# Transposing V by 32-bit words in the backward part of a fused decode block

## The chip, the cores and the metric

The kernel runs on one core of a Trainium2 chip (trn2). The metric is the device time of one execution in microseconds. Engines are named as in the profile: PE is TensorE (PEld its weight loads), DVE is VectorE, ACT is ScalarE, POOL is GpSimd, SP is SyncE, which here issues nearly all DMAs.

## What is computed

A decode step of one transformer block, forward and backward: layer norm, attention over a cache, output projection, layer norm, gated MLP. There are 4 batch rows and 32 attention heads, so 128 pairs of row and head, called heads here and numbered s. Each has a K and a V cache of 4096 x 128 in bf16, 1 MB each. The outputs are the block's output and the gradients of x, of both caches and of the weights. What matters here, for one head:

```
forward:   p  = softmax(q K^T * scale)          # 1 x 4096
           o  = p V
backward:  dP = dO V^T                          # 1 x 4096
           dS = p * (dP - dO.o) * scale
           dK = dS^T q      (4096 x 128, written out)
           dV = p^T dO      (4096 x 128, written out)
```

K is read once, V twice (once forward, once backward), and dK and dV are written once.

## The kernel before

SBUF holds one large tile, the arena, of 23 slots of 4160 bf16 elements for each of 128 partitions. A slot holds a head of K, of V, or of a gradient: 4096 tokens as 128 partitions of 32 tokens, with 128 features each. Slots are taken from a list of free ones when a load or a gradient is set up and given back when it is used or stored. All loads and stores of caches go through SP's queue in the order in which the program writes them.

**Forward, to 660 us.** A loop over 64 groups of 2 heads loads K and V, computes scores and softmax, and builds the sums that the backward needs. It is not touched.

**Middle, 660 to 700 us.** Projection, MLP and their backward for the 4 rows. It ends with dO for the first 8 attention heads (dOT_bf, features on partitions, one column for each head; `dO_columns`, L768, and `dO_rows`, L778) and the first transposes of V (`V_T`, L793).

**Backward, from 700 us.** The first SP = 32 heads are taken one by one (`front`, L1212), the other 96 in NT = 48 pairs (`front_pair`, L1292). In a pair, two heads of one batch row lie in two neighbouring slots, 64 partitions for each head, 64 tokens on a partition, and are loaded with one DMA of 2 MB. For a head or a pair:

1. V is loaded again (`load_V2` L829, `load_pair` L1276).
2. V is transposed on PE in 128 x 128 blocks, one token number of all partitions at a time. Eight blocks fill one PSUM tile, pt_tps, of 128 x 1024 bf16, one bank; one ACT copy takes it back to the same place in SBUF (L800 and L801, L1298 and L1299). psT has two such tiles. A head takes 4 banks, a pair 8.
3. dP comes from matmuls with 32 output rows and 512 columns, four side by side in the array (`tile_position`); the stationary operand is zero but for the column or columns with dO (`zd` for heads, `zt` for pairs), so that each head adds its rows to a shared PSUM tile, dP_ps (L1228, L1313). `dO_window` (L1191) and `dO_pair` (L1287) write dO into zd and zt on POOL, two heads or pairs ahead. After the matmuls the slot of V is given back.
4. After four heads, or two pairs, `rows_out` (L1200, ACT) and `rows_T` (L1205, four f32 transposes on PE) bring dP_ps back to tokens on partitions, in the midst of the next front. `group_dS` (L1239) and `group_dS_pair` (L1319) form dS on DVE.
5. dV and dK are outer products on DVE (L806 for heads, L1379 for pairs) into free slots, and each is stored. Their factors are P or dS, doubled, and dO or q copied to all partitions. The doubled P is made on POOL (`P_pairs` L1195, `P2_pair` L1372), the copies on PE and ACT (`replicate` L1172, `replicate_pair` L1356).

The order is written out by hand in the loops from L1436 on: fronts run 5 heads (L) or 3 pairs (LP) ahead of dK, and dV runs some heads ahead of dK (`more_V`, `lead_V`). Between them `side` (L1428) places the rest: dO of the other heads, dq, the weight gradients (`grad_unit`, L981). SP meets loads and stores in this order and waits at each for its slot or its data.

The two matmul loops for dP take the transposed V like this (L1228 and L1313):

```
lhsT=zq_window(zd[hl], 2 * hl + u), rhs=VT[:, j0:j0 + 4, :]
lhsT=zt[t % B][:, 32 - m:64 - m],   rhs=v[:, j0:j0 + 4, :]
```

Of the kernel before, what the change touches and what calls it, by code (L numbers as in the profile page):

```python
# [9 lines left out]
FP32 = mybir.dt.float32  # L10
BF16 = mybir.dt.bfloat16
# [10 lines left out]
SP = 32  # L22
# [5 lines left out]
def kernel(  # L28
# [22 lines left out]
    nc = tc.nc  # L51
    P = nc.NUM_PARTITIONS

    B = A_x.shape[0]
# [3 lines left out]
    Dh = A_k_cache.shape[3]  # L58
    F = B_w1.shape[1]
    NH = B * H  # L60
# [4 lines left out]
    SJ = Sk // P  # L65
    FC = F // P
    GW = 8
# [13 lines left out]
    while f0 < F:  # L81
        w = min(512, F - f0)
# [125 lines left out]
    for i in range(2):  # L208
        t = fcon.tile([P, 64], BF16, name=f"onesw{i}")
# [132 lines left out]
    def zq_window(z, m):  # L342
        a = 66 * (m % 2) + 32 + (m % 2) - m
        return z[:, a:a + 32]
# [305 lines left out]
    for gi in range(NGI):  # L650
        nxt = gi < NGI - 1
        a, na, nb = gi * G, gi * G + 2, gi * G + 3
# [137 lines left out]
    V2s, VTs = {}, {}  # L790


    def V_T(s, ps, part=range(SJ // GW)):  # L793
        if s not in VTs:
            VTs[s] = V2s.pop(s)
        v = VTs[s].heads()
        for g in part:
            pt = ps.tile([P, GW, P], BF16, tag="tps", name="pt_tps")
            for i in range(GW):
                nc.tensor.transpose(pt[:, i, :], v[:, g * GW + i, :], ident_b[:])  # L800
            nc.scalar.copy(out=v[:, g * GW:(g + 1) * GW, :], in_=pt[:])  # L801

    P2s, first_gv = {}, []

# [160 lines left out]
    with ExitStack() as c2:  # L965
# [218 lines left out]

        rows = {}
        dS2s = {}
        zd = [bw3.tile([P, 132], BF16, name=f"zd{i}", tag=f"zd{i}", bufs=1) for i in range(B)]
        for i in range(B):
            nc.gpsimd.memset(zd[i][:], 0.0)

        def dO_window(s):  # L1191
            if s < SP:
                nc.gpsimd.tensor_copy(out=zd[s % B][:, 32:132:67], in_=dOT_bf[:, s:s + 1].to_broadcast([P, 2]))

        def P_pairs(s):  # L1195
            if s < SP and s not in P2s:
# [15 lines left out]
        def front(s):  # L1212
            hl = s % B
            if s not in VTs:
                for g in range(SJ // GW):
                    V_T(s, psT, range(g, g + 1))
                    if hl == 0 and g == 0:
                        rows_out()
                    if hl == 0 and g == 2:
                        rows_T()  # L1220
            VT = VTs[s].heads()
            if hl == 0:
                rows["acc"] = psD.tile([P, 512], FP32, tag="dP", name="dP_ps")
            dO_window(s + 2)
            for u in range(2):
                for c in range(4):
                    j0 = 8 * c + 4 * u
                    nc.tensor.matmul(rows["acc"][32 * c:32 * (c + 1), :], lhsT=zq_window(zd[hl], 2 * hl + u),  # L1228
                                     rhs=VT[:, j0:j0 + 4, :], start=(hl == 0 and u == 0),
                                     stop=(hl == B - 1 and u == 1), tile_position=(0, 32 * c))  # L1230
            if hl == B - 1:
                rows["ps"] = rows.pop("acc")
            sl = VTs.pop(s)
            if nv["next"] < SP and len(V2s) + len(VTs) + len(vring) < NV2:
                vring.append(sl.i)
            else:
                gave(sl.i, stored=False)

        def group_dS(g):  # L1239
            i0 = g * B  # L1240
            T = rows.pop("T").rearrange("p jj (c m) -> p c m jj", c=4)
            t = rows.pop("t")[:, 0:B * SJ].rearrange("p (b j) -> p b j", b=B)
            t5 = t.rearrange("p b (c u jj) -> p b c u jj", c=4, u=2)
            for hl in range(B):
                nc.vector.tensor_scalar(out=t5[:, hl], in0=T[:, :, 2 * hl:2 * hl + 2, :], scalar1=c_rep[:, i0 + hl:i0 + hl + 1],
                                        scalar2=scale, op0=ALU.subtract, op1=ALU.mult)
# [40 lines left out]
        def dO_pair(t):  # L1287
            if t < NT:
                s, s2 = two(t)
                nc.gpsimd.tensor_copy(out=zt[t % B][:, 32:34], in_=dOT_bf[:, s:s2 + 1:B])  # L1290

        def front_pair(t, mid):  # L1292
            pl = t % 2
            v = pV[t].t[:, 0:2 * SJ * Dh].rearrange("p (j d) -> p j d", d=Dh)
            for g in range(2 * SJ // GW):
                pt = psT.tile([P, GW, P], BF16, tag="tps", name="pt_tps")
                for i in range(GW):
                    nc.tensor.transpose(pt[:, i, :], v[:, g * GW + i, :], ident_b[:])  # L1298
                nc.scalar.copy(out=v[:, g * GW:(g + 1) * GW, :], in_=pt[:])  # L1299
                if pl == 0 and g == 0:  # L1300
                    rows_out()
                if pl == 0 and g == 2:
                    rows_T()
                if g == 3:
                    mid()
            if pl == 0:
                rows["acc"] = psD.tile([P, 512], FP32, tag="dP", name="dP_ps")
            dO_pair(t + 2)
            for u in range(4):
                m = 8 * pl + 2 * u  # L1310
                for c in range(4):
                    j0 = 16 * c + 4 * u
                    nc.tensor.matmul(rows["acc"][32 * c:32 * (c + 1), :], lhsT=zt[t % B][:, 32 - m:64 - m], rhs=v[:, j0:j0 + 4, :],  # L1313
                                     start=(pl == 0 and u == 0), stop=(pl == 1 and u == 3), tile_position=(0, 32 * c))
            if pl == 1:
                rows["ps"] = rows.pop("acc")
            pV.pop(t).give()

        def group_dS_pair(g):  # L1319
            T = rows.pop("T").rearrange("p jj (c z l u a) -> p z l a c u jj", c=4, z=2, l=2, u=4, a=2)  # L1320
            t = rows.pop("t")[:, 0:4 * SJ].rearrange("p (l j) -> p l j", l=2)
            t5 = t.rearrange("p l (c u jj) -> p l c u jj", c=4, u=4)
            for l in range(2):
                for a, s in enumerate(two(2 * g + l)):
                    r_ = slice(64 * a, 64 * (a + 1))
                    nc.vector.tensor_scalar(out=t5[r_, l], in0=T[r_, 0, l, a], scalar1=c_rep[r_, s:s + 1],  # L1326
                                            scalar2=scale, op0=ALU.subtract, op1=ALU.mult)
            pdS[g] = bw3.tile([P, 2, 2 * SJ, 2], BF16, tag="dS2", name="dS2", bufs=1)
            nc.vector.tensor_tensor(out=pdS[g][:], in0=t[:, :, :, None].to_broadcast([P, 2, 2 * SJ, 2]),
                                    in1=P_two(2 * g)[:, :, :, None].to_broadcast([P, 2, 2 * SJ, 2]), op=ALU.mult)  # L1330

        Pp, zt, P2b = {}, [], []

        def P_two(t, n=2):
# [2 lines left out]
        def P_rows(q):  # L1337
            if q >= NT // B or q in Pp:
                return
            if not Pp:  # L1340
                Pp["s"] = Slot("Pp")
                x = Pp["s"].t[:, NT * 2 * SJ:]
                zt.extend(x[:, 66 * i:66 * (i + 1)] for i in range(B))
                nc.gpsimd.memset(x[:, 0:66 * B], 0.0)
                P2b.extend(x[:, n:n + 4 * SJ].rearrange("p (j t) -> p j t", t=2) for n in (66 * B, 66 * B + 4 * SJ))
# [82 lines left out]
        def side(s):  # L1428
# [4 lines left out]
            elif s >= O0:  # L1433
                step("q")

        for s in range(2):  # L1436
            dO_window(s)
        for s in range(3, 6):
# [11 lines left out]
        for s in range(SP):  # L1450
# [73 lines left out]
```

## Time and profile before

| | |
|---|---|
| median of 3 runs | 1697.81 us (1697.64 to 1698.8) |
| span of the profiled execution, first to last instruction | 1696.2 us |
| PE busy, matmuls / weight loads | 1233.4 us (73%) / 943.4 us, 16,228 of each |
| DVE, ACT, POOL busy | 1234.4 us (73%), 959.5 us (57%), 336.9 us (20%) |
| moved by DMA | 707.45 MB, 417 GB/s in the mean |
| transposes of V, pairs (L1298) | 3,072 of 128 x 128, 308.1 us, mean 272 ns |
| their copies (L1299) | 384 of 128 x 1024, 369.8 us, mean 1023 ns |
| transposes of V, heads (L800), copies (L801) | 1,024, mean 229 ns; 128, mean 1025 ns |
| dP matmuls, pairs (L1313), heads (L1228) | 768, mean 484 ns; 256, mean 403 ns |
| f32 transposes in rows_T (L1210) | 128, mean 370 ns; their weight loads 196 ns |
| POOL copies of dO (L1290, L1193) | 48, mean 995 ns; 32, mean 872 ns |

The profile is one execution recorded by the hardware. The span is all of it that has rows; 1.6 us lie between it and the median of the runs. Its page gives busy times by engine, 40 slices of the span, the DMA queues, the chain that ended last, and groups of instructions by source line. A row of a group reads: line, engine, operation, what it writes and reads, shape, count, then busy time and mean of one, then the idle time of the engine before them and who ended it. Slice digits are tenths. The trace behind it also has each DMA packet with queue, start, duration and size, and the landings: every transfer on SP's queue is split over 16 DMA engines, and each reports the end of its share.

### The profile page before, as it was taken

The numbers are of one execution on the slowest core, as the hardware profiler recorded it, in microseconds if no ns is written. First come the engines' busy times: TensorE is split into PE (matmuls) and PEld (weight loads), VectorE is DVE, ScalarE is ACT, GpSimd is POOL, SyncE is SP. The second block draws the span as 40 slices with busy tenths as digits, with TensorE's granted clock in tenths as the row PEclk, the third lists the DMA queues.
The fourth block names the chain that finished last, engine by engine and source line by source line (L and its number), as shares of the span: only waits on it lengthen the run. The fifth ranks groups of instructions, "written<-read, shape, count | busy, mean of one in ns | idle before, by whom it ended". The sixth has DMA issues, their size and how long they took to land.

```text
span 1696.2 us, 37839 instructions
## 1 busy us (share of the span) xinstructions
PE 1233.4 (73%) x16228; PEld 943.4 (56%) x16228; DVE 1234.4 (73%) x1198; ACT 959.5 (57%) x1490; POOL 336.9 (20%) x583
## 2 busy tenths in 40 slices
PE   5889888888888888877876755667665666766650
PEld 4777667666677666655655544444444444444440
DVE  5989999999998997667766466575665655655683
ACT  3555544454454544677665555666665666666650
POOL 1211222222222222222231121011210102011120
PEclk8999999999999999899898689886678777676675
DMA  9999999999999999999999999999999999999995
GB/s 401 424 424 424 424 424 424 424 424 423 416 423 406 424 414 397 395 414 425 425 425 429 428 429 428 429 430 429 429 429 428 418 430 429 422 418 425 415 429 230
DMA packets 81000, 707.45 MB, mean 417 GB/s; under 512 B 8748, under 2 KB 12984, under 8 KB 15296
## 3 DMA queue, kind: packets, MB, share of 16 engines
q1 hardware_dynamic: 80416, 704.94, 99.0%
q8 instruction: 127, 2.08, 0.5%
q14 instruction: 41, 0.34, 0.0%
q0 software_dynamic: 416, 0.10, 0.0%
HBM read 422.59 MB, written 282.34 MB: 416 GB/s over the span
## 4 chain that ended last, share of the span: by engine, by line
DMA 46%; DVE 9%; PE 3%; issue 2%; ACT 1%; DVEq 0%; POOL 0%; SPq 0%; ACTq 0%
DMA out_dram<-arena 43%; DVE arena L1379 7%; DMA arena<-in_A_v_cache_dram 3%; DVE arena L806 1%; PE M_ps L472 1%; DVE arena L457 1%; PE pt_w L601 0%; ACT arena L1299 0%; ACT Pn L436 0%; DVEq L1519 0%; PE kP_ps L482 0%; DVE dPr L1326 0%; PE pt_tps L1298 0%; PE gu_ps L873 0%; PE dn_ps L904 0%
## 5 line engine op out<-in xcount | busy, mean ns | idle before, releaser
L1299 ACT COPY arena<-pt_tps 128x1024 bf16<-128x1024 bf16 x384 | 369.8, 1023 | 232.3 <-PE pt_tps L1298 231.6
L1298 PE MATMUL pt_tps<-ident_b,arena 128*128 128x128 bf16 x3072 | 308.1, 272 | 204.7 <-DMA arena<-in_A_v_cache_dram 149.4
L1298 PEld LDWEIGHTS <-arena 128*128 128x128 bf16 x3072 | 263.9, 125 | 304.2 <-DMA arena<-in_A_v_cache_dram 172.8
L1379 DVE TENSOR_TENSOR arena<-arena 128x8192 bf16<-128x8192 bf16 x48 | 212.5, 4427 | 205.1 <-DMA out_dram<-arena 202.3
L472 PE MATMUL M_ps<-arena 128*128 128x130 bf16 x4096 | 285.1, 222 | 42.9 <-DMA arena<-in_A_v_cache_dram 42.2
L457 DVE TENSOR_TENSOR arena<-arena 128x4096 bf16<-128x4096 bf16 x128 | 292.5, 2285 | 23.9 <-POOL arena L453 23.9
L472 PEld LDWEIGHTS <-arena 128*128 128x128 bf16 x4096 | 251.9, 99 | 64.0 <-DMA arena<-in_A_v_cache_dram 57.2
L1379 DVE TENSOR_TENSOR arena<-dS,arena 128x8192 bf16<-128x8192 bf16 x48 | 212.3, 4424 | 73.0 <-DMA out_dram<-arena 73.0
L364 DVE STREAM_TRANSPOSE arena<-arena 128x512 f32<-128x512 f32 (+1 forms) x321 | 250.7, 797 | 0.0
L359 ACT COPY arena<-pt_tps 128x1024 bf16<-128x1024 bf16 x128 | 129.5, 1012 | 188.9 <-PE pt_tps L358 150.5
L1376 POOL COPY arena<-arena 128x128 bf16<-128x128 bf16 x48 | 55.3, 1153 | 492.3 <-ACT arena L1353 286.3
L370 POOL TENSOR_TENSOR W<-qrep,wmask 128x128 bf16<-128x128 bf16 x128 | 120.2, 939 | 85.6 <-PE S_ps L390 70.8
L801 ACT COPY arena<-pt_tps 128x1024 bf16<-128x1024 bf16 x128 | 121.7, 1025 | 26.1 <-PE pt_tps L800 24.8
L453 POOL COPY arena<-P_all 128x64 bf16<-128x64 bf16 x128 | 32.7, 255 | 412.8 <-ACT P_all L447 409.8
L806 DVE TENSOR_TENSOR arena<-dS,arena 128x4096 bf16<-128x4096 bf16 x32 | 73.2, 2293 | 35.0 <-DMA out_dram<-arena 34.7
L800 PE MATMUL pt_tps<-ident_b,arena 128*128 128x128 bf16 x1024 | 78.5, 229 | 27.1 <-ACT arena L801 27.1
L1313 PE MATMUL dP_ps<-arena 128*32 128x512 bf16 x768 | 85.7, 484 | 7.6 <-ACT arena L1299 7.3
L800 PEld LDWEIGHTS <-arena 128*128 128x128 bf16 x1024 | 67.2, 104 | 37.5 <-issue 35.9
L447 ACT COPY P_all<-pt_P 32x64 bf16<-32x64 bf16 x256 | 52.1, 204 | 53.6 <-PE pt_P L443 51.4
L806 DVE TENSOR_TENSOR arena<-P,arena 128x4096 bf16<-128x4096 bf16 x29 | 66.4, 2295 | 19.8 <-DMA out_dram<-arena 19.8
L358 PE MATMUL pt_tps<-ident_b,arena 128*128 128x128 bf16 x1024 | 80.1, 222 | 0.0
L482 PE MATMUL kP_ps<-arena,onesw 128*32 128x512 bf16 x1024 | 79.6, 388 | 0.0
(245 smaller groups left out, 1576.5 us busy)
## 6 DMA issues: line engine op xcount, KB each, us to landing
out_dram<-arena SPq DMA_DIRECT2D x96, 2048.0 KB, 27.9
arena<-in_A_v_cache_dram SPq DMA_DIRECT2D x160, 1024.0 KB, 15.9
arena<-in_A_k_cache_dram SPq DMA_DIRECT2D x128, 1024.0 KB, 15.3
arena<-in_A_v_cache_dram SPq DMA_DIRECT2D x48, 2048.0 KB, 32.1
out_dram<-arena SPq DMA_DIRECT2D x72, 1024.0 KB, 20.2
arena<-in_A_wq_dram SPq DMA_DIRECT2D x8, 1024.0 KB, 14.4
arena<-in_B_w_dram SPq DMA_DIRECT2D x8, 896.0 KB, 15.3
out_dram<-arena SPq DMA_DIRECT2D x6, 896.0 KB, 28.4
```

Source lines behind the costliest of these rows:

```text
L359: nc.scalar.copy(out=KT[:, c * GW:(c + 1) * GW, :], in_=pt[:])
L364: nc.vector.transpose(out=KT[:, c * w_:(c + n) * w_], in_=Kn[:, c * w_:(c + n) * w_])
L370: nc.gpsimd.tensor_tensor(out=W[:, hl], in0=qrep[:, :, s:s + 1].to_broadcast([P, 4, 32]), in1=wmask[:, hl, None, :].to_broadcast([P, 4, 32 ...
L457: nc.vector.tensor_tensor(out=PK[:, :, 0:Dh].rearrange("p j (r t) -> p j r t", t=2), in0=Ks[s].heads().rearrange("p j (r t) -> p j r t", t=2),
L472: nc.tensor.matmul(hold["M"][:], lhsT=Vn[:, j, :], rhs=PK[:, j, :], start=(j == 0), stop=(j == SJ - 1))
L800: nc.tensor.transpose(pt[:, i, :], v[:, g * GW + i, :], ident_b[:])
L801: nc.scalar.copy(out=v[:, g * GW:(g + 1) * GW, :], in_=pt[:])
L806: nc.vector.tensor_tensor(out=dst.rearrange("p j (r t) -> p j r t", t=2), in0=col2[:, :, None, :].to_broadcast([P, SJ, Dh // 2, 2]), in1=r ...
L1298: nc.tensor.transpose(pt[:, i, :], v[:, g * GW + i, :], ident_b[:])
L1299: nc.scalar.copy(out=v[:, g * GW:(g + 1) * GW, :], in_=pt[:])
L1313: nc.tensor.matmul(rows["acc"][32 * c:32 * (c + 1), :], lhsT=zt[t % B][:, 32 - m:64 - m], rhs=v[:, j0:j0 + 4, :], start=(pl == 0 and u == ...
L1379: nc.vector.tensor_tensor(out=dst.rearrange("p (j r t) -> p j r t", r=Dh // 2, t=2), in0=col2[:, :, None, :].to_broadcast([P, 2 * SJ, Dh / ...
```

## The change

V is no longer transposed as bf16 blocks but as 32-bit words. A word is two neighbouring features of one token. A 128 x 128 f32 transpose takes two neighbouring tokens at once (64 words each), and moves the words as they are; the identity is `ident_f`, which the kernel already has. Four such transposes fill the same PSUM bank that eight filled before, seen as f32, and the same ACT copy takes it to the same place as bf16. Afterwards partition 64 i + r holds features 2 r and 2 r + 1 of token i of a couple, side by side in the row.

dP is therefore summed over even and odd features in two matmuls (k = 0, 1), whose moving operand steps over every other element (`words_of`). The number of dP matmuls stays: 8 for a head, 16 for a pair. The stationary operand needs the even or the odd features of dO, on partitions 0 to 63 for the first token of a couple and 64 to 127 for the second. `dO_words` makes them: four small matmuls with every other column of the identity and one ACT copy, once for the 32 single heads (`dOw`) and once for the other 96 (`zt[B]`). `dO_window` and `dO_pair` copy from there, in two copies of 64 partitions in place of one of 128; zd and zt get a new shape. The rows of dP come in another order, which `group_dS` and `group_dS_pair` follow with other strides and the same number of instructions.

The core of the diff:

```diff
+    def words_T(ps, v, g):
+        w = v.bitcast(FP32).rearrange("p (x r) -> p x r", r=Dh)
+        pt = ps.tile([P, GW, P], BF16, tag="tps", name="pt_tps")
+        ptw = pt.rearrange("p a b -> p (a b)").bitcast(FP32).rearrange("p (x q) -> p x q", q=P)
+        for jj in range(4):
+            nc.tensor.transpose(ptw[:, jj, :], w[:, 4 * g + jj, :], ident_f[:])
+        nc.scalar.copy(out=v.rearrange("p (j d) -> p j d", d=Dh)[:, g * GW:(g + 1) * GW, :], in_=pt[:])
+
+    def words_of(v, g, k):
+        return v.rearrange("p (x r t) -> p t x r", r=Dh, t=2)[:, k, 4 * g:4 * g + 4]
...
-            for i in range(GW):
-                nc.tensor.transpose(pt[:, i, :], v[:, g * GW + i, :], ident_b[:])
-            nc.scalar.copy(out=v[:, g * GW:(g + 1) * GW, :], in_=pt[:])
+            words_T(ps, VTs[s].t[:, 0:SJ * Dh], g)
...
-        zd = [bw3.tile([P, 132], BF16, name=f"zd{i}", tag=f"zd{i}", bufs=1) for i in range(B)]
+        zd = [bw3.tile([P, 2, 32], BF16, name=f"zd{i}", tag=f"zd{i}", bufs=1) for i in range(B)]
+        dOw = bw3.tile([P, 2, SP], BF16, name="dOw", tag="dOw", bufs=1)
...
+        def dO_words(dst, s0, s1):
+            ps = psrep.tile([P, 2, s1 - s0], FP32, tag="rep", name="dOw_ps")
+            for k in range(2):
+                for i in range(2):
+                    nc.tensor.matmul(ps[64 * i:64 * (i + 1), k, :], lhsT=ident_b[:, k:P:2], rhs=dOT_bf[:, s0:s1],
+                                     start=True, stop=True, tile_position=(0, 64 * i))
+            nc.scalar.copy(out=dst, in_=ps[:])
+
         def dO_window(s):
             if s < SP:
-                nc.gpsimd.tensor_copy(out=zd[s % B][:, 32:132:67], in_=dOT_bf[:, s:s + 1].to_broadcast([P, 2]))
+                for i in range(2):
+                    r_ = slice(64 * i, 64 * (i + 1))
+                    nc.gpsimd.tensor_copy(out=zd[s % B][r_, :, 2 * (s % B) + i], in_=dOw[r_, :, s])
...
-            for u in range(2):
+            for k in range(2):
                 for c in range(4):
-                    j0 = 8 * c + 4 * u
-                    nc.tensor.matmul(rows["acc"][32 * c:32 * (c + 1), :], lhsT=zq_window(zd[hl], 2 * hl + u),
-                                     rhs=VT[:, j0:j0 + 4, :], start=(hl == 0 and u == 0),
-                                     stop=(hl == B - 1 and u == 1), tile_position=(0, 32 * c))
+                    nc.tensor.matmul(rows["acc"][32 * c:32 * (c + 1), :], lhsT=zd[hl][:, k, :], rhs=words_of(v, c, k),
+                                     start=(hl == 0 and k == 0), stop=(hl == B - 1 and k == 1), tile_position=(0, 32 * c))
...
-                nc.gpsimd.tensor_copy(out=zt[t % B][:, 32:34], in_=dOT_bf[:, s:s2 + 1:B])
+                for i in range(2):
+                    r_ = slice(64 * i, 64 * (i + 1))
+                    nc.gpsimd.tensor_copy(out=zt[t % B][r_, :, ZP + 2 * i:ZP + 2 * i + 2], in_=zt[B][r_, :, s - SP:s2 - SP + 1:B])
...
-            for u in range(4):
-                m = 8 * pl + 2 * u
-                for c in range(4):
-                    j0 = 16 * c + 4 * u
-                    nc.tensor.matmul(rows["acc"][32 * c:32 * (c + 1), :], lhsT=zt[t % B][:, 32 - m:64 - m], rhs=v[:, j0:j0 + 4, :],
-                                     start=(pl == 0 and u == 0), stop=(pl == 1 and u == 3), tile_position=(0, 32 * c))
+            for u in range(2):
+                m = 16 * u + 4 * pl
+                for k in range(2):
+                    for c in range(4):
+                        nc.tensor.matmul(rows["acc"][32 * c:32 * (c + 1), :], lhsT=zt[t % B][:, k, ZP - m:ZP - m + 32],
+                                         rhs=words_of(v, 2 * c + u, k), start=(pl == 0 and u == 0 and k == 0),
+                                         stop=(pl == 1 and u == 1 and k == 1), tile_position=(0, 32 * c))
...
+        dO_words(dOw[:], 0, SP)
         for s in range(2):
             dO_window(s)
...
                 if s + L == SP:
+                    dO_words(zt[B], SP, NH)
                     dO_pair(0)
                     dO_pair(1)
```

`front_pair` replaces its own transposes by `words_T(psT, v, g)` in the same way.

More of the change, by code (lines that the diff above doesn't have):

```diff
@@ L795, in V_T @@
             VTs[s] = V2s.pop(s)
-        v = VTs[s].heads()
         for g in part:
-            pt = ps.tile([P, GW, P], BF16, tag="tps", name="pt_tps")
-            for i in range(GW):
-                nc.tensor.transpose(pt[:, i, :], v[:, g * GW + i, :], ident_b[:])
-            nc.scalar.copy(out=v[:, g * GW:(g + 1) * GW, :], in_=pt[:])
+            words_T(ps, VTs[s].t[:, 0:SJ * Dh], g)
     P2s, first_gv = {}, []
@@ L1220, in front @@
                         rows_T()
-            VT = VTs[s].heads()
+            v = VTs[s].t[:, 0:SJ * Dh]
             if hl == 0:
@@ L1240, in group_dS @@
             i0 = g * B
-            T = rows.pop("T").rearrange("p jj (c m) -> p c m jj", c=4)
+            T = rows.pop("T").rearrange("p jj (c m) -> p c jj m", c=4)
             t = rows.pop("t")[:, 0:B * SJ].rearrange("p (b j) -> p b j", b=B)
-            t5 = t.rearrange("p b (c u jj) -> p b c u jj", c=4, u=2)
+            t5 = t.rearrange("p b (c jj i) -> p b c jj i", c=4, i=2)
             for hl in range(B):
-                nc.vector.tensor_scalar(out=t5[:, hl], in0=T[:, :, 2 * hl:2 * hl + 2, :], scalar1=c_rep[:, i0 + hl:i0 + hl + 1],
+                nc.vector.tensor_scalar(out=t5[:, hl], in0=T[:, :, :, 2 * hl:2 * hl + 2], scalar1=c_rep[:, i0 + hl:i0 + hl + 1],
                                         scalar2=scale, op0=ALU.subtract, op1=ALU.mult)
@@ L1289, in dO_pair @@
                 s, s2 = two(t)
-                nc.gpsimd.tensor_copy(out=zt[t % B][:, 32:34], in_=dOT_bf[:, s:s2 + 1:B])
+                for i in range(2):
+                    r_ = slice(64 * i, 64 * (i + 1))
+                    nc.gpsimd.tensor_copy(out=zt[t % B][r_, :, ZP + 2 * i:ZP + 2 * i + 2], in_=zt[B][r_, :, s - SP:s2 - SP + 1:B])
         def front_pair(t, mid):
             pl = t % 2
-            v = pV[t].t[:, 0:2 * SJ * Dh].rearrange("p (j d) -> p j d", d=Dh)
+            v = pV[t].t[:, 0:2 * SJ * Dh]
             for g in range(2 * SJ // GW):
[L1296 to L1299, printed above, removed]
+                words_T(psT, v, g)
                 if pl == 0 and g == 0:
@@ L1319, in group_dS_pair @@
         def group_dS_pair(g):
-            T = rows.pop("T").rearrange("p jj (c z l u a) -> p z l a c u jj", c=4, z=2, l=2, u=4, a=2)
+            T = rows.pop("T").rearrange("p jj (g z l i a) -> p z l a g jj i", g=8, z=2, l=2, i=2, a=2)
             t = rows.pop("t")[:, 0:4 * SJ].rearrange("p (l j) -> p l j", l=2)
-            t5 = t.rearrange("p l (c u jj) -> p l c u jj", c=4, u=4)
+            t6 = t.rearrange("p l (g jj i) -> p l g jj i", g=8, i=2)
             for l in range(2):
@@ L1325, in group_dS_pair @@
                     r_ = slice(64 * a, 64 * (a + 1))
-                    nc.vector.tensor_scalar(out=t5[r_, l], in0=T[r_, 0, l, a], scalar1=c_rep[r_, s:s + 1],
+                    nc.vector.tensor_scalar(out=t6[r_, l], in0=T[r_, 0, l, a], scalar1=c_rep[r_, s:s + 1],
                                             scalar2=scale, op0=ALU.subtract, op1=ALU.mult)
@@ L1330, in group_dS_pair @@
                                     in1=P_two(2 * g)[:, :, :, None].to_broadcast([P, 2, 2 * SJ, 2]), op=ALU.mult)
+        ZP = 20
         Pp, zt, P2b = {}, [], []
@@ L1342, in P_rows @@
                 x = Pp["s"].t[:, NT * 2 * SJ:]
-                zt.extend(x[:, 66 * i:66 * (i + 1)] for i in range(B))
-                nc.gpsimd.memset(x[:, 0:66 * B], 0.0)
-                P2b.extend(x[:, n:n + 4 * SJ].rearrange("p (j t) -> p j t", t=2) for n in (66 * B, 66 * B + 4 * SJ))
+                n = 2 * (ZP + 32)
+                zt.extend(x[:, n * i:n * (i + 1)].rearrange("p (k c) -> p k c", k=2) for i in range(B))
+                nc.gpsimd.memset(x[:, 0:n * B], 0.0)
+                n *= B
+                zt.append(x[:, n:n + 2 * (NH - SP)].rearrange("p (k c) -> p k c", k=2))
+                n += 2 * (NH - SP)
+                P2b.extend(x[:, n + i * 4 * SJ:n + (i + 1) * 4 * SJ].rearrange("p (j t) -> p j t", t=2) for i in range(2))
             Pp[q] = True
```

## Prediction, made before the result was known

> **What bounds the kernel now.** I read the page from the slices down, then the last stretch by windows, then the waits, and last the records of the single DMA packets in the trace.
>
> ```profile
> DMA  9999999999999999999999999999999999999995
> GB/s 401 424 424 424 424 424 424 424 424 423 416 423 406 424 414 397 395 414 425 425 425 429 428 429 428 429 430 429 429 429 428 418 430 429 422 418 425 415 429 230
> ...
> q1 hardware_dynamic: 80416, 704.94, 99.0%
> q8 instruction: 127, 2.08, 0.5%
> ```
>
> The 16 DMA engines are busy from the first slice to the last but one. PE, DVE and ACT are busy 73, 73 and 57% of the span, and what they save is worth nothing unless it reaches the DMA. Only the last slice is not full, so I looked there.
>
> ```profile
> 1650.00:1676.00 26.00, 1.18 (x9) 0.46 (x8) 16.68 (x9) 0.59 (x1) 0.00 (x0) 0.55 0.97 413
> 1676.00:1696.00 20.00, 0.00 (x0) 0.00 (x0) 0.00 (x0) 0.00 (x0) 0.00 (x0) 0.50 0.07 30
> ```
>
> The columns are the window, PE, PEld, DVE, ACT, POOL, clock, DMA share and GB/s. In the last 20 us no engine computes, and the DMA share is 0.07, about one sixteenth: **one DMA engine works alone.** The packet records say the same. The last store's sixteen parts land at 1674.6 to 1677.6 us, but for one, at 1694.9. Followed back through the landings, this engine is 1.7 us behind the next one at 850 us, 5.6 at 1000, 10.0 at 1200, 14.8 at 1450 and 17.3 from 1650 on. It is never idle; it needs longer for its share. Its eight 16 KB packets of a 2 MB transfer should take 4.86 us. They do in a V load (mean 4.91, 48 loads), but in a store they took 5.07 (91 stores), and the excess goes with the instructions recorded meanwhile. From 1610 us on, in stretches of 5 us, 77 ns went with 39 instructions, 176 with 105, 236 with 99, 20 with 7, 259 with 103 and 3 with 4. From 820 to 1676 us it lost 24.2 us in 132 stores, in which 8,513 PE instructions were recorded. That is 2.8 ns for each if PE bears all of it, and 1.9 if a fit gives ACT, DVE, POOL and SP their parts. PE's busy time explains it less well than the count, and adds nothing beside the other engines' counts. So the end is set by one slow DMA engine, and it is slow by the number of instructions that run while it stores.
>
> **What the change removes.** The transposes of V are 3,072 (L1298, 48 pairs) and 1,024 (L800, 32 heads). Half of them go, 2,048, each with its weight load: 4,096 PE instructions.
>
> Term 1, the slow engine. Of the records of L1298, 5,867 of 6,144 fall in its stores, and of L800's 1,407 of 2,048, for the transposes start when a load has landed. Half of 7,274 is 3,637; by 1.9 ns it is 6.9 us, by 2.8 ns 10.2. I take 2.3 ns, as the fit leaves scatter: **-8.4 us**. The engine is 17.3 us behind the next, so all of this shows at the end.
>
> Term 2, instruction loading. q8's 2.08 MB in 127 packets of 16 KB are PE's 32,456 instructions at 64 bytes, 256 to a packet. 4,096 less some 24 new ones are 16 packets. One takes 0.98 us of an engine (124.5 us by 127), and the landings show one engine after another pushed back by about that: one packet for each of 16 engines, **-1.0 us**.
>
> **What it adds or moves.** *PE time.* A bank takes four f32 transposes for eight bf16 ones. Before has f32 128x128 transposes in L1210, next to L1298 and at the same clock:
>
> ```profile
> 1565.43 1.01 PE L1298 MATMUL pt_tps<-ident_b,arena 128*128 128x128 bf16 x8 [0.25 <-ACT arena L1299]
> 1566.23 1.06 PE L1210 MATMUL dPT_ps<-ident_f,dPr 128*128 128x128 f32 x4
> ```
>
> So a bank costs 1.06 us where it cost 1.01 (0.66 and 0.61 at full clock, at 1625 us). The copy that empties it stays 128x1024 bf16, 1.02 us (L1299, L801), and sets the pace of a front as before. For +0.05 us by 512 banks, 26 us of PE, the cover is PE's wait for V (149.4 us at L1298); if it were gone, that would be the price.
>
> The Trainium skill, "TensorE: Matmul & The Clock Gate", section "Weight-path perf modes", speaks against f32 here: it says that the fast weight load is not used for FP32. The trace has 196 ns for an f32 load (L1210) and 125 for a bf16 one (L1298); four of the one against eight of the other are 0.78 against 1.00 us, so the rule holds for one load and not for a bank, and the sum stays.
>
> *dP.* Pair: 16 matmuls of 512 columns as before, head: 8, but the moving rows step by two elements. L390 has both kinds side by side:
>
> ```profile
> L390 PE MATMUL S_ps<-arena,W 128*32 128x256 bf16 x1536 | 74.7, 284 | 0.8 <-DVE arena L364 0.6
> L390 PE MATMUL S_ps<-arena,zq 128*32 128x256 bf16 x512 | 68.2, 276 | 0.2 <-ACT arena L359 0.2
> ```
>
> W's columns step by two, zq's do not: 8 ns in 276. By 1,024 matmuls of twice the width that is 16 us at most, overlapped four at a time, hidden as above. The order of the groups awaited is unchanged. group_dS moves strides only: 283 ns (L1326) and 244 (L1245), in a DVE that waits 275 us for stores at L1379.
>
> *The new dO_words, twice.* Four small matmuls and one ACT copy (0.19 us for 32 columns, 0.37 for 256) at 700 us. PE has then ended c_ps at 699.9 and ACT its copy at 700.6, while POOL is busy until 702.2 with the cast and the fills. So it is covered but for POOL's own two extra copies, 0.155 us each, ahead of the first dP and two more ahead of L806 at 703.2, which waits for POOL. The DMA share is 0.80 at 705 to 710 us, so that 0.6 us passes through: **+0.6 us**. The second one, at head 27, has two pairs to hide behind.
>
> *POOL.* Each dO_window (32) and dO_pair (48) becomes two copies: 80 more by 0.87 to 0.99 us, POOL from 337 to some 413 us of 1,696. Queued behind them are the P pairs for DVE (L1198, L1376). DVE waited 2.9 us in all for L1376, PE once, 2.5 us, for zd. I put **+0.2 us**, bounds 0 and +1.5.
>
> Sum: -8.4 - 1.0 + 0.6 + 0.2 = -8.6 us. The profiled execution's span is 1696.2 us, 1.6 us (0.1%) below the median of the runs, 1697.81; I take the difference to the median: **1689 us**.
>
> **Rivals.** *No difference to be measured* (within 0.2%, 3.4 us, about what a measurement of this kernel can tell from no change). The 2 to 3 ns could belong to the bytes that PE reads or that ACT writes, which stay. For it: counts and busy time rise together, and a fit in the early stage, 700 to 900 us, does not part them. It could also be that executions that are only timed don't carry this load. Against it: the fit later, and 1696.2 against 1697.81. Then -1.0 + 0.8: 1697.6.
>
> The Trainium skill has such a lag too: "DMA: Bandwidth & Descriptors", section "Latency and other measured facts", says two of the engines are usually slower, and guesses at the rings of software-issued DMAs. Those move 0.10 MB here (q0), and the lag grows all the same; by that rule nothing would change but term 2, 1697 us.
>
> *Slower, by f32 transposes that don't overlap.* If four end to end take 4 x 370 ns (L1210's mean), a bank takes 1.48 us, over the copy's 1.02, and PE becomes the bound of a front. It decides in the first five fronts, 702 to 740 us, where V loads wait for dP to free a slot (10.4 us in three waits of SP) and the DMA is not full: 5 x 4 banks by 1.48 less 0.92, the present step, is 11 us, and without term 1 the time is 1708 us. It counts from the point where a bank exceeds 1.02 us. The two rows at 1565 us speak against it.
>
> *That it does not do what it says*, four transposes being split in two passes each, would leave the records where they were: 1697.6, counted with no difference.
>
> **How the numbers follow.** Forecast 0.68, no difference 0.23, slower 0.09. The forecast's own range is 1685 (4,096 by 2.8 ns, and term 2) to 1692 (6.9 and 1.0, less 1.5 and 0.6). The range must take in the second case and leave out the third: 1685 to 1699. Faster by over 0.2% 0.68, within 0.23, slower 0.09.
>
> **What would show it.** After: q8 at some 111 packets; PE at about 14,190 matmuls; 2,048 f32 transposes near the present time for a bank, the copies still 1.02 us; the stretch with a DMA share of 0.07 down from about 18 us to about 9; the full part of the DMA ending where it did. I am wrong if the lone engine's stretch is as long as before, if DMA share falls under 0.95 between 700 and 1650 us, or if ACT waits longer for pt_tps than 231.6 us at L1299 by more than the 26 us above.

## The result, and the profile after

The changed kernel takes 1688.44 us (median of 5 runs, 1687.49 to 1690.15) against 1697.81 us (median of 5, 1696.46 to 1698.8): a ratio of 0.9945, 95% interval 0.9933 to 0.9957. It is 9.4 us faster; the forecast was 8.8. The profiled execution took 1688.41 us, its span 9.6 us less than before.

The page of the changed kernel, the lines that answer to those shown of before:

```profile
span 1686.6 us, 33967 instructions
...
PE 1260.6 (75%) x14188; PEld 924.3 (55%) x14188; DVE 1233.9 (73%) x1198; ACT 960.9 (57%) x1492; POOL 379.6 (23%) x663
...
DMA  9999999999999999999999999999999999999996
GB/s 400 424 424 424 425 423 425 424 424 421 418 423 411 424 411 397 398 410 426 425 426 428 429 429 429 431 430 429 429 430 430 429 429 431 430 429 431 430 429 259
...
q1 hardware_dynamic: 80416, 704.94, 99.2%
q8 instruction: 112, 1.84, 0.4%
```

The bytes of the transfers (q1) are the same and the DMA engines are as full as before. PE runs 2,040 matmuls fewer, yet is busy for longer: 1260.6 us against 1233.4. What differs is how fast the DMA moves: from the 32nd slice on, four slices of before show 415 to 422 GB/s; those of after stay between 429 and 431 up to the last.

The end by windows (window, PE, PEld, DVE, ACT, POOL, clock, DMA share, GB/s):

```profile
1640.00:1666.00 26.00, 2.43 (x22) 0.84 (x20) 18.27 (x9) 1.97 (x3) 0.00 (x0) 0.63 1.00 427
1666.00:1676.00 10.00, 0.00 (x0) 0.00 (x0) 0.00 (x0) 0.00 (x0) 0.00 (x0) 0.50 0.36 152
1676.00:1686.60 10.60, 0.00 (x0) 0.00 (x0) 0.00 (x0) 0.00 (x0) 0.00 (x0) 0.50 0.05 22
```

One engine still works alone at the end, with a share of 0.05. But the full part of the DMA now ends near 1670 us, where it ended near 1676 before. So the whole DMA came forward, and the lone stretch only shrank.

The landings of the 530 SP transfers, which come in the same order in both kernels, say where. Up to 700 us those of the last engine agree within half a microsecond. From 840 us on the last engine gains steadily: 1.3 us at 912, 4.0 at 1170, 7.0 at 1440, 9.6 at the end. The eighth of the sixteen gains 5.6 us, most of it after 1000, and the first 8.4, all of it after 1300. The last stands 12.2 us behind the one ahead of it (before 17.3) and 14.4 behind the eighth (before 18.3).

The groups of the changed part, from the lines of the profile:

```profile
L799 ACT COPY arena<-pt_tps 128x1024 bf16<-128x1024 bf16 x512 | 491.7, 1023 | 249.0 <-PE pt_tps L798 247.3 <-issue 1.3
L798 PE MATMUL pt_tps<-ident_f,arena 128*128 128x128 f32 x2048 | 410.7, 356 | 202.9 <-DMA arena<-in_A_v_cache_dram 125.6 <-ACT arena L799 77.1
L1328 PE MATMUL dP_ps<-arena 128*32 128x512 bf16 x768 | 84.4, 471 | 8.4 <-ACT arena L799 8.3
```

and two banks of one pair in the timeline (start, duration):

```profile
1564.31 2.03 PE L798 MATMUL pt_tps<-ident_f,arena 128*128 128x128 f32 x8 [0.25 <-ACT arena L799]
...
1565.46 1.93 ACT L799 COPY arena<-pt_tps 128x1024 bf16<-128x1024 bf16 x2 [0.29 <-PE pt_tps L798]
```

Eight f32 transposes take 2.03 us, 1.02 for a bank, beside copies at 0.97 each: they overlap, and the copy still sets the pace. The strided rows of dP cost nothing (471 ns, before 484).

### The profile page after: what moved, and what is told of

It reads as the page before. It is cut to its first block, busy times and chain, and to the rows that moved or that the text cites. A ratio compares the mean times of both kernels' runs of the same rounds, so it can differ in the third digit from the quotient of the medians.

```text
span 1686.6 us, 33967 instructions
## 1 busy us (share of the span) xinstructions
PE 1260.6 (75%) x14188; PEld 924.3 (55%) x14188; DVE 1233.9 (73%) x1198; ACT 960.9 (57%) x1492; POOL 379.6 (23%) x663
## 4 chain that ended last, share of the span: by engine, by line
DMA 35%; DVE 7%; ACT 5%; PE 5%; issue 3%; DVEq 0%; SPq 0%; POOL 0%; ACTq 0%
DMA out_dram<-arena 34%; DVE arena L1400 7%; ACT arena L799 5%; PE pt_tps L798 1%; PE dq_ps L1007 1%; PE dP_ps L1245 1%; DMA arena<-in_A_v_cache_dram 1%; PE pt_wo L610 0%; DVEq L1542 0%; PE rep_ps L1186 0%; DVE dPr L1342 0%; ACT dPr L1221 0%; PE dOT_ps L773 0%; PE dPT_ps L1228 0%; PE c_ps L784 0%
## 5 line engine op out<-in xcount | busy, mean ns | idle before, releaser
L799 ACT COPY arena<-pt_tps 128x1024 bf16<-128x1024 bf16 x512 | 491.7, 1023 | 249.0 <-PE pt_tps L798 247.3
L798 PE MATMUL pt_tps<-ident_f,arena 128*128 128x128 f32 x2048 | 410.7, 356 | 202.9 <-DMA arena<-in_A_v_cache_dram 125.6
L798 PEld LDWEIGHTS pt_tps<-ident_f,arena 128*128 128x128 f32 x2048 | 304.1, 182 | 349.3 <-issue 191.6
L472 PE MATMUL M_ps<-arena 128*128 128x130 bf16 x4096 | 286.9, 223 | 30.0 <-DMA arena<-in_A_v_cache_dram 29.2
L472 PEld LDWEIGHTS <-arena 128*128 128x128 bf16 x4096 | 254.6, 99 | 49.6 <-DMA arena<-in_A_v_cache_dram 42.5
L1397 POOL COPY arena<-arena 128x128 bf16<-128x128 bf16 x48 | 43.7, 912 | 432.7 <-ACT arena L1374 200.0
L1308 POOL COPY arena<-arena 64x4 bf16<-64x4 bf16 x96 | 68.8, 717 | 136.3 <-PE dP_ps L1328 108.6
L358 PE MATMUL pt_tps<-ident_b,arena 128*128 128x128 bf16 x1024 | 80.8, 224 | 0.0
L422 ACT ACTIVATE E<-S_ps,nm 128x256 f32<-128x256 f32 x64 | 30.4, 474 | 82.7 <-DVE nm L419 82.6
L991 PE MATMUL gps<-arena 4*128 4x512 bf16 x110 | 47.3, 452 | 39.0 <-ACT arena L985 39.0
## 6 DMA issues: line engine op xcount, KB each, us to landing
arena<-in_A_wq_dram SPq DMA_DIRECT2D x8, 1024.0 KB, 14.3
```

The lines of the kernel that those rows point to most:

```text
L358: nc.tensor.transpose(pt[:, i, :], Kn[:, c * GW + i, :], ident_b[:])
L472: nc.tensor.matmul(hold["M"][:], lhsT=Vn[:, j, :], rhs=PK[:, j, :], start=(j == 0), stop=(j == SJ - 1))
L798: nc.tensor.transpose(ptw[:, jj, :], w[:, 4 * g + jj, :], ident_f[:])
L799: nc.scalar.copy(out=v.rearrange("p (j d) -> p j d", d=Dh)[:, g * GW:(g + 1) * GW, :], in_=pt[:])
```

## The experiments

Two theories stand. **Count:** each instruction that runs while the DMA stores costs the slow engine 2 to 3 ns, and as it turned out the others some time too. **Something else that moved:** PE's busy time, the form of dP, the copies on POOL, or the early transfers. Where nothing else is said, a kernel is the changed one with one edit, timed beside the kernel before on the same chip; its difference to "after" is that to 1688.44 us, which was measured on another occasion. The kernel before had medians of 1697.88 to 1698.09 us beside these runs and 1697.81 beside "after".

### 1. The kernel before once more

> The kernel before, once more. It shows what repeats of the first profile. Theory (one DMA engine is slow by the number of instructions that run while it stores): its lag at the end is again 17 to 18 us behind the next engine, a stretch with a DMA share of about 0.07 of 18 us, and the excess of the stores is again 2 to 3 ns for each recorded PE instruction. If the lag was an accident of that execution, it differs by more than 5 us. The bursts of long packets on all engines (62 us of engine time more before than after, 3.9 us for each engine) should be here again if they belong to the kernel, and lie at other places or be missing if they do not.

1698.03 us (one run), span 1696.3. The last engine ends 17.1 us behind the next, and loses 23.9 us in its stores. The drops of the whole DMA come at the same places (1305 to 1345, 1475 to 1495, 1535, 1565, 1600 us): 174 packets of 16 KB over 200 ns late, 70 us in all, where the trace of before has 180 with 75 us and that of after 31 with 13. They belong to the kernel and are no accident of one run. PE is busy for 1250.4 us in this profile and for 1233.4 in the first: the same program's PE total repeats only to some 17 us.

### 2. The instructions given back, without their work

```diff
+        for jj in range(4):
+            nc.tensor.matmul(ptw[:, 0, 0:1], lhsT=ident_b[:], rhs=ident_b[:, 0:1], start=True, stop=True)
         for jj in range(4):
             nc.tensor.transpose(ptw[:, jj, :], w[:, 4 * g + jj, :], ident_f[:])
```

> The changed kernel with four matmuls of one column added ahead of the transposes of each bank (512 banks: 2,048 matmuls, each with a weight load of 128 columns), written to PSUM places that the transposes then overwrite; the result is unchanged. PE gets back the 4,096 instructions that the change took away, but nothing else of it is undone. Theory of the count: 3,637 of 4,096 fall in stores, by 2.3 ns, and 16 packets of instructions: +8.4 +1.0, so 1698 us (1696 to 1700), with the lone engine's lag back to about 17 us. Rival, that the gain came with the words themselves (fewer columns read by PE, another order): no more than +1.0 for the packets, 1689.5 us.

1697.09 us (1695.46 to 1699.73), ratio 0.9998 [0.9989, 1.0007]: 8.7 us over after for 4,096 instructions (2,048 one-column matmuls and their weight loads), 2.1 ns for each, and the gain is gone. The lag returns (16.7 us behind the next), the stores' loss (22.9 us) and the bursts too (145 packets, 58 us). That is the count's side.

### 3. The same instructions in the forward part

```diff
+            for _ in range(16):
+                nc.tensor.matmul(hold["M"][:, 0:1], lhsT=ident_b[:], rhs=ident_b[:, 0:1], start=True, stop=True)
```

ahead of the L472 group of each of the 128 heads, where the DMA only loads.

> The changed kernel with the same 2,048 matmuls of one column and their weight loads, but in the forward part, 16 ahead of each head's 32 matmuls of L472, where the DMAs only load. The result is unchanged. Theory of the count in stores: no engine is slower in loads, only the 16 packets of instructions, 1.0 us for each engine: 1689.4 us (1688 to 1691). Rival, that each instruction costs DMA time wherever it runs: +8 to +10 us, 1698 us. Should PE become the bound of the forward part (busy 84% there), the DMA share falls below 0.95 before 660 us and the run tells nothing of either.

1692.95 us (1692.12 to 1694.41), ratio 0.997 [0.9958, 0.9982], 4.5 us over after: between the two numbers, so both were off. The DMA share stays at 1.00 to 1.01 up to 700 us, so PE did not become the bound there. The landings of the profiled execution, the slowest of the six (1694.41 us), part the 4.5 us: 3 to 4 us have come by 760 us, to all engines alike, without growth of the lag (1.1 us behind the eighth, after 2.1); 15 instruction packets more explain 0.9 of them. So loads lose time to instructions too, 2 to 3 us here. The rest, up to 3 us more, comes later, most of it after 1000 us, where nothing was added, with 92 late packets. Why these follow stays open.

### 4. Relieving the slow engine directly

Two late stores of dK, pairs NT-4 and NT-3, were issued as two DMAs each, of 120 and of 8 partitions.

```diff
-            nc.sync.dma_start(out=two_heads(out_ap, t), in_=g_.t[:, 0:2 * SJ * Dh])
+            o_ = two_heads(out_ap, t)
+            for a_, b_ in ((0, 120), (120, P)) if out_ap is out_2 and t in (NT - 4, NT - 3) else ((0, P),):
+                nc.sync.dma_start(out=o_[a_:b_, :], in_=g_.t[a_:b_, 0:2 * SJ * Dh])
```

> The changed kernel with two of the last stores of dK (2 MB each, pairs NT-4 and NT-3) issued in two pieces, partitions 0 to 119 and 120 to 127. A store of 128 partitions is split over 16 DMA engines; 120 rows can be split over 15 and 8 over 8, so that one engine may be left out of these two stores. Theory that one slow engine sets the end: if the one left out is the slow one, the end comes two shares of 4.86 us earlier, 1688.4 - 9.7 = 1679 us, and the lone stretch at the end shrinks to some 3 us. If another is left out, nothing or up to +1.2 us. Rival, that the end is set by compute or by all engines together: no gain, 1688 to 1690 us.

1700.07 us (1699.04 to 1700.82), ratio 1.0011 [1.0003, 1.002]: 11.6 us over after, a miss. The windows of this kernel show it where the two stores are:

```profile
1640.00:1665.00 25.00, 1.55 (x17) 0.52 (x8) 17.43 (x9) 1.10 (x2) 0.00 (x0) 0.62 0.99 338
```

The engines are all busy, and yet move 338 GB/s where after moved 427: 16 KB packets took 775 ns in the mean from 1650 to 1664 us, after 612. Their median is 611 ns in both: some packets took far longer, not all a little. The lag grew from 15 us behind the eighth to 24, and was 21 at the last store. Which engine got which rows the trace does not say, so this says nothing on the lag's cause; it shows that two stores cut in 120 and 8 partitions are slower stores, and not which of the two pieces makes them so.

### 5. The bf16 transposes put back, dP kept

```diff
-        for jj in range(4):
-            nc.tensor.transpose(ptw[:, jj, :], w[:, 4 * g + jj, :], ident_f[:])
+        vv = v.rearrange("p (x r t) -> p x r t", r=Dh, t=2)
+        for i in range(GW):
+            nc.tensor.transpose(pt[:, i, :], vv[:, 4 * g + i // 2, :, i % 2], ident_b[:])
...
-        return v.rearrange("p (x r t) -> p t x r", r=Dh, t=2)[:, k, 4 * g:4 * g + 4]
+        return v.rearrange("p (x t r) -> p t x r", r=Dh, t=2)[:, k, 4 * g:4 * g + 4]
```

> The changed kernel with the transposes alone put back: eight 128x128 bf16 transposes per bank, of the even and then of the odd features of four block pairs, into the same bank and with the same copy; dP still sums over even and odd features, now over contiguous rows. So 2,048 transposes and as many weight loads come back, and everything else of the change stays. By the theory of the instruction count the whole gain goes with them: 1697.5 us (1696 to 1699), 127 or 128 instruction packets, the last engine some 17 us behind the next. If the gain came with the form of dP or of the copies on POOL, the time stays at 1688 to 1690.

1698.79 us (1697.72 to 1700.85), ratio 1.0007 [0.9998, 1.0015]. All of the gain was in the transposes; dP summed over even and odd features (over contiguous rows here), the words of dO and the copies on POOL, all still there, brought nothing. The page of this kernel:

```profile
PE 1241.7 (73%) x16236; PEld 952.5 (56%) x16236; DVE 1234.9 (73%) x1198; ACT 960.0 (57%) x1492; POOL 388.0 (23%) x663
...
GB/s 401 424 425 424 424 424 425 423 420 424 419 422 409 424 413 397 392 413 425 425 425 429 428 428 429 429 429 430 428 429 428 419 428 430 420 426 425 415 426 232
...
q8 instruction: 127, 2.08, 0.5%
```

PE is busy 18.9 us less than in after, and the kernel is 10.4 us slower, so it is not PE's busy time. (By run 1 a difference of 18.9 us is hardly more than scatter; that PE was not busier is enough.) The dips are back in the same slices as before (419, 420, 415).

### 6. A quarter of the count, more work

```diff
+        nc.tensor.matmul(ptw[:, 0:2, :], lhsT=ident_b[:], rhs=v[:, 1024 * g:1024 * g + 256], start=True, stop=True)
```

> The changed kernel with one 256-column bf16 matmul ahead of the four transposes of each of the 512 banks, whose result is written over: 512 matmuls and 512 loads, 1,024 PE instructions more, each matmul some 0.15 to 0.25 us, 80 to 125 us of PE busy time, about what the 2,048 one-column matmuls of the earlier run added (129 us) at a quarter of their count. By the count: a quarter of 8.65 us, 1690.6 us (1689.5 to 1691.5). By PE's busy time (8.65 us for 129 us): 1694 to 1697.

1691.48 us (1689.97 to 1692.92), ratio 0.9961 [0.9948, 0.9973]: 3.0 us for 1,024 instructions. The added group here, and that of the one-column matmuls in run 2:

```profile
L797 PE MATMUL pt_tps<-arena,ident_b 128*128 128x256 bf16 x512 | 161.4, 315 | 195.4 <-DMA arena<-in_A_v_cache_dram 128.5 <-ACT arena L800 64.8
```

```profile
L798 PE MATMUL pt_tps<-ident_b 128*128 128x1 bf16 x2048 | 129.2, 167 | 50.8 <-ACT arena L801 46.2
```

By their own groups, 161 us of matmuls cost 3.0 us where 129 us of them cost 8.7. But matmuls overlap, and PE's total says less; the pages of this run and of run 2:

```profile
PE 1264.5 (75%) x14700; PEld 958.4 (57%) x14700; DVE 1234.5 (73%) x1198; ACT 963.9 (57%) x1492; POOL 387.8 (23%) x663
```

```profile
PE 1312.6 (77%) x16236; PEld 996.4 (59%) x16236; DVE 1233.5 (73%) x1198; ACT 969.1 (57%) x1492; POOL 379.1 (22%) x663
```

Against after's 1260.6 us PE is busy 3.9 us longer here and 52 in run 2, so that by the total this run alone does not tell the count from the busy time. Run 5, where PE was busy for less and the kernel was slower, does, and so does run 9 below. The 3.0 us are not evenly spread either: in the profiled execution the last engine is 2.1 us later than in after by 800 us, and falls only 0.9 us further behind from there to the end.

### 7. Half of the count

Run 2 with two one-column matmuls per bank (`range(2)`).

> The changed kernel with two one-column matmuls ahead of the four transposes of each bank, 1,024 matmuls and 1,024 loads, half of what the earlier run with four added. If the cost goes with the count in proportion, 1692.8 us (1691.5 to 1694), the last engine about 14.5 us behind the next. If a part of it comes only above some rate of instructions, as the bursts in which all engines slow down may, only the lag's half, 1690.5 us (1690 to 1691.5).

1692.85 us (1692.67 to 1693.84), ratio 0.997 [0.9959, 0.9981]: 4.4 us for 2,048 instructions, half of run 2. So the cost is proportional between these two runs. In its parts it is less even: the last engine ends 15.1 us behind the next, and late packets are 96 with 40 us.

### 8. The same count on POOL

```diff
+    pz = const.tile([P, 2], BF16, name="pz")
...
+        for jj in range(8):
+            nc.gpsimd.memset(pz[0:1, 0:1], 0.0)
```

> The changed kernel with eight one-element fills on POOL ahead of the transposes of each of the 512 banks, 4,096 POOL instructions more and none on PE. If any recorded instruction costs the DMA what one of PE does, the time goes back to 1697 us (1695 to 1699), with the last engine 16 us or more behind the next. If only PE's count, the time is that of the changed kernel but for some 16 more instruction packets, 1689.4 us (1688.5 to 1690.5). If the fills delay the P pairs behind them on POOL, DVE shows it in its waits for POOL, and the DMA share falls.

1712.86 us (1711.76 to 1714.44), ratio 1.0087 [1.0074, 1.0101]: above every number named. The landings were already 7.9 us late at 700 us, ahead of the first fill. The edit had a second effect: the small tile lies ahead of the arena and moves it by 32 bytes. Two runs part this.

### 9. The count on POOL, with the arena on its boundary

As run 8, with `pz` 64 elements (128 bytes) wide.

> The run with eight fills on POOL per bank once more, with the tile that they write made 128 bytes wide instead of 4. The small tile had moved the arena, where all transfers land, by 32 bytes, from a multiple of 128 to one of 32; this one moves it by 128. If the move cost the 7.9 us by which the transfers of that run were already late at 700 us, ahead of the first fill, they are late by nothing there now. From then on, 4,096 POOL instructions more: by the theory that any recorded instruction costs the storing engine what one of PE does, 8.7 us, so 1697 us; by the growth of the last engine's delay in the earlier run after 760 us (15.3 us), if none of that came from the move, 1703 us; if POOL's instructions cost nothing, 1688 to 1690 us.

1700.73 us (1699.94 to 1702.4), ratio 1.0016 [1.0007, 1.0025]. The lateness at 700 us is gone (2.3 us early instead). 12.3 us over after is 3.0 ns for each of the 4,096 instructions, none of them on PE; but the fair comparison is with run 10, the same tile without the fills (1686.41 us): 14.3 us, 3.5 ns. Run 8 against the same 32 bytes without fills gives 14.2 us. The fills, and the line of the page on which PE's total stays that of after (1260.6):

```profile
L800 POOL MEMSET pz<- 1x1 bf16 x4096 | 375.6, 92 | 230.1
...
PE 1262.2 (74%) x14188; PEld 921.7 (54%) x14188; DVE 1234.9 (73%) x1198; ACT 960.4 (57%) x1492; POOL 702.8 (41%) x4759
```

The last engine ends 20.5 us behind the eighth and late packets are 260 with 113 us. PE's instruction packets (q8) are 112, as in after, so none of this is their loading. One thing is not clean: DVE now waits for POOL's fills, ahead of the stores:

```profile
DVE arena L1404 <- POOL pz L800: 88.6, 19, 10.1
```

The DMA share stays at 1.00 to 1.01 between 740 and 1676 us, so this wait let no DMA engine run dry; whether it shifts what meets what, and so makes a part of the 3.5 ns, is not tested.

### 10. The arena's place alone

An unused tile ahead of the arena, with one fill of one element, of 4, 128 and 384 bytes.

```diff
+    pz = const.tile([P, 2], BF16, name="pz")
+    nc.gpsimd.memset(pz[0:1, 0:1], 0.0)
```

> The changed kernel with nothing but a 4-byte tile and one fill of it ahead of the arena, which moves the arena by 32 bytes, off the multiples of 64 and 128. If the move alone made the transfers of the forward part slower (8 KB packets of 313 ns in the run with the fills, 309 otherwise), the transfers are 7.9 us late at 700 us, and the time is 1696 to 1700 us, depending on whether stores suffer too. If it did not, 1688.4 us.

> The changed kernel with nothing but an unused tile of 128 bytes (one fill of one element) ahead of the arena: the arena moves by 128 bytes, from 30336 to 30464, a multiple of 256. In the run with the fills on POOL and this same tile, transfers landed 2.0 to 2.4 us earlier at 705 us, ahead of the first fill. If the move did that, 1686.3 us; if chance in the waits of that run did, 1688.4 us; if only multiples of 64 matter, as the move by 32 suggests, 1688.4 us too.

> As the move by 128 bytes, but by 384, so that the arena begins at 30720, a multiple of 1024. Its slots are 8320 bytes apart, so that only the first of them keeps this. If the boundary of 64 bytes is the only one that matters, 1688.4 us (1687.5 to 1689.5); if larger ones help, below 1686.3 us.

By 32 bytes, to 30368: 1698.64 us (1697.91 to 1699.04), ratio 1.0003 [0.9994, 1.0012]. An unused tile costs as much as the whole change gains. Its page:

```profile
GB/s 398 417 420 418 419 418 419 419 416 418 415 415 413 418 400 394 395 407 426 425 426 428 429 429 430 430 428 430 430 430 429 429 432 428 431 431 428 429 427 251
```

In the forward, which only loads, 418 instead of 424; where stores join, the full rate. An 8 KB packet took 313 ns there in the median, 309 otherwise.

By 128 and by 384 bytes: 1686.41 us (1686.2 to 1687.31), ratio 0.9934 [0.992, 0.9948], and 1686.37 us (1685.83 to 1687.03), ratio 0.9932 [0.992, 0.9945]. Both medians are 2 us below after, and these are the fastest kernels here; the intervals overlap with that of after, and neither was timed side by side with after. Their landings lead after's by 1.1 to 1.4 us at 800 us and by 2.3 to 2.5 in the last engine at the end; the 16 KB instruction packets of the forward took some 970 ns, after's 1010. How the arena's place changes these is open.

### The runs side by side

The last two columns are of one profiled execution each.

| kernel | instructions added in the backward | time, us | last engine behind the eighth at the end, us | time over 611 ns of all 16 KB packets, 900 to 1640 us |
|---|---|---|---|---|
| after | 0 | 1688.44 | 14.4 | 26 us |
| 6, wide | 1,024 PE | 1691.48 | 16.9 | 33 |
| 7, half | 2,048 PE | 1692.85 | 16.4 | 59 |
| 2 | 4,096 PE | 1697.09 | 18.4 | 85 |
| 5, bf16 transposes | 4,096 PE | 1698.79 | 18.7 | 97 |
| before | 4,080 PE, 80 fewer on POOL | 1697.81 | 18.3 | 102 |
| 9, POOL (1686.41 without the fills) | 4,096 POOL | 1700.73 | 20.5 | 143 |

## Why the prediction was right, and which step was off

**Term 1, the slow engine: right in kind, 1.2 us too large, and not all of the story.** It was to lose 8.4 us less in its stores. It lost 24.2 us in 132 stores before and 17.0 in 134 after: 7.2 us less. That the count explains it and PE's busy time does not is borne out by runs 2, 5, 7 and 9, and run 9 shows that PE is not special. That loads hardly suffer holds for this engine in the backward: its 48 shares of 2 MB V loads took 4.91 us in the mean before and 4.88 after. In the forward, run 3 shows a loss in loads too.

**The step that failed: the excess was put on one engine alone, "the full part of the DMA ending where it did" and the lone stretch going down to about 9 us.** What the slow engine saved did all show at the end, as the prediction said, for it was still the last. But its lag to the next fell to 12.2 us only, by 5.1, because the other engines came forward too. The time over 611 ns of all 16 KB packets was 102 us before and is 26 after; 76 by 16 is 4.8 us for each engine, and the eighth ended 5.6 us earlier. Most of it lies in bursts of late packets, which stand in the GB/s line of before (418, 422, 418, 415), and the prediction read past them. That the sum came out within 1 us is in part luck: of the last engine's 9.6 us, 7.2 are in stores (8.4 forecast), 0.9 are instruction packets, and some 1.5 are not placed by these counts, while nothing is left at the end of the 0.8 us that the start and POOL were to cost. The range of 1685 to 1699 us would have held a kernel with no difference as well; what the result bears out is its middle, 1689.

**Term 2, instruction loading:** 15 packets fewer (127 to 112), 16 forecast; by 0.97 us of an engine and 16 engines 0.9 us. Right.

**PE time:** a bank measured 1.02 us (forecast 1.06, before 1.01), hidden. ACT's wait for pt_tps is 247.3 us for 512 banks; before it was 231.6 for 384 and 24.8 for 128, so it fell by 9.1 where up to 26 more were allowed for. The Trainium skill's "TensorE: Matmul & The Clock Gate", section "Weight-path perf modes", which denies FP32 the fast load, agrees with the rows for one load (182 ns here, 121 for the bf16 load of run 5). A bank needs half as many f32 loads, though, and so less time for them (0.73 us for four against 0.97 for eight).

**The start:** 0.5 us late at 705 us, as forecast, but made good by 760 us. **POOL:** 43 us more instead of 76 (the copies of dO_pair took 717 ns, not 870 to 990), and no wait that tells.

**The rivals.** No difference, because the cost goes by bytes or busy time: out by the result and runs 5 and 9. Transposes that don't overlap: out by the timeline. Transposes split in two: out by the page, which counts 14,188 matmuls. The Trainium skill's "DMA: Bandwidth & Descriptors", section "Latency and other measured facts", guesses that the rings of software DMAs cause such a lag, and by that the time would have been 1697; q0 moves 0.10 MB in all these kernels while the lag goes from 14.4 to 20.5 us with the count, so the rings do not set its size here.

**Open:** what an instruction takes from the DMA. Every run here with a span has its instructions recorded, so none tells the instruction from its recording, and a cost of the recording would look the same. Why the last engine suffers most, and why the late packets come in bursts at fixed places, was not found either.

## What to carry to other kernels

Where the DMA is full from end to end, look at how it ends, engine by engine, and at dips in its rate while its share is full; in these recorded runs both went with the mere number of instructions, and then fewer and larger ones pay though their engine gets busier. Price such a cost by adding empty instructions in two amounts (4.4 us for 2,048, 8.7 for 4,096) before redesigning anything. And when a test adds a tile, see where it moves the others: here a 4-byte tile cost 10 us and spoiled a test.

## What was not expected of the hardware

- The place of the arena: 30336, 30464 and 30720 bytes (multiples of 128) gave 1688.4, 1686.4 and 1686.4 us; 30368 (a multiple of 32 only) 1698.6. No other start was tried, so where the boundary lies is not shown. The loss arose where the DMA only loads: 8.4 us by 705 us and only 1.6 more in the last engine after.
- Instructions cost more where the DMA stores, placement where it only loads: 4,096 PE instructions cost 8.7 us in the storing part; in the loading part 3 to 4 us at once, 0.9 of it instruction packets. 4,096 one-element fills on POOL cost 14.3 us.
- A DMA share of 1.00 is no proof of full rate: 338 GB/s at a share of 0.99 with two stores cut in 120 and 8 partitions, 427 with stores of 128.
